# Banded attention, first batch: the mask is put into the PSUM banks by a product with the identity

## The chip, the cores and the metric

One NeuronCore of a Trainium2 chip runs the whole program. The metric is the device time of one execution in microseconds (us). PE is TensorE (its weight loads are shown apart as PEld), DVE is VectorE, ACT is ScalarE, POOL is GpSimd; SP issues every DMA.

## The reference

Inputs: `q`, `k`, `v` of 4 batches, 8 heads, 576 positions, 64 values per head, and the weights of two gated layers. In fp32, with scale 1/8:

```
out_d     = softmax(scale * q_d k_d^T) v_d          # q, k, v averaged over groups of 4 positions: 144 positions
out_up    = each row of out_d repeated 4 times
scores    = scale * q k^T, and -1e9 where |i - j| >= 4
out_local = softmax(scores) v                       # softmax: subtract the row's maximum, exp, divide by the sum
x   = (out_up + out_local), heads side by side      # 2304 x 512
x   = (sigmoid(x w_gate) * (x w_val)) w_out         # layer 1, 512 -> 1536 -> 512
h   = x w_in ;  y = (h * sigmoid(1.702 h)) w_out    # layer 2, 512 -> 2048 -> 512
```

## The kernel before

The kernel records operations (`op`: engine, assumed duration, function, what it reads and writes, a due time) and a planner (`Plan.order`) then lists them. It keeps a clock for each engine, takes the operation of the earliest due time among those whose inputs it believes ready, and so fixes the order in which each engine executes. Each engine works strictly in that order; semaphores make it wait for data. Where the planner believes TensorE idle at the start, it puts in fillers (`warm`, 128x128 bf16 products into a bank that nobody holds, L1173), until the first products of the gated layer's second half. PSUM banks for the attention are handed out by the planner when the first operation that writes one is listed, and given back when its last reader is done. In the first batch six banks serve (`pa` x2, `acc` x4); later batches have only the two `pa`.

**Attention** goes in 16 jobs, one for a batch and a pair of heads; jobs 0 to 3 are the first batch. A job has five parts:

- *scores* (L525): 576 queries lie as 24 tiles of 24 (+8) queries, each against 30 keys; 48 small fp32 products fill two banks (one per head) with 128 x 6 x 30 scores. DVE adds the mask out of SBUF into `sc`, one bank at a time (L532), takes the maximum over both heads (L540), subtracts it (L541); ACT takes exp (L543); DVE sums, divides and transposes into `tt` (L544 to L552).
- *down* (L565): the scores of the averaged positions (`qd`, `kd` from POOL, L493 and L495) in two more banks, maximum on DVE (L572), exp on ACT (L580) and division (L594) into `pd`.
- *down_t* (L609): TensorE transposes `pd`, ACT copies it to `pdt` (L614).
- *values* (L637, L645): products with `v`; ACT copies the averaged part to `up` (L652); DVE adds the two parts into `xf` (L666); ACT and then POOL split it into two fp32r parts, `xhi` and `xlo` (L672, L675). Values read `v` as `vt` (banded) and `vd`, which DVE averages from `vg` (L462, L464), once for two jobs.

**Gated layer 1** then takes x of one batch at a time (L787 to L789, three products for one fp32 product: hi·hi, hi·lo, lo·hi). The weights come packed as 512 KB transfers, are unpacked by ACT and DVE (`we`, L699 to L708) and split into `whi` (ACT, L717) and `wlo` (DVE or POOL, L719). A gated product over one quarter of d_model needs x of one job, so the first block of 128 hidden columns is 4 quarters x 2 matrices x 3 = 24 products of 512 columns, and needs all four jobs. This visit of batch 0 runs beside the attention of batch 1, and so on; layer 2 follows.

The mask is made by POOL at the start, before any recorded operation (L368 to L378). The first operation of the plan for TensorE before the change is job 0's scores.

Of the kernel before, what the change touches and what calls it, by code (L numbers as in the profile page):

```python
# [10 lines left out]
F32 = mybir.dt.float32  # L11
BF16 = mybir.dt.bfloat16
# [5 lines left out]
AX = mybir.AxisListType  # L18

P = 128  # L20
# [41 lines left out]
class Plan:  # L62
# [29 lines left out]
    def op(self, eng, ns, fn, reads=(), writes=(), due=0.0, after=0.0):  # L92
        o = Op()
        o.eng, o.ns, o.fn, o.due, o.n, o.ready = eng, ns, fn, due, len(self.ops), after
        o.fresh, o.bufs = [], set()
        deps = set()
        for group, writing in ((reads, False), (writes, True)):
            for x in group:
                b, part = x if isinstance(x, tuple) else (x, None)
                assert b.some or b.slot.last is b  # L100
                if b.some:
                    o.bufs.add(b)
                    if not b.log:
                        o.fresh.append(b)
                new = True
                for p, q, w in b.log:
                    if (w or writing) and (part is None or q is None or part == q):
                        deps.add(p)
                        new = new and not w
                if new:  # L110
                    for x in b.before:
                        deps.update(e[0] for e in x.log)
        for group, writing in ((reads, False), (writes, True)):
            for x in group:
                b, part = x if isinstance(x, tuple) else (x, None)
                b.log.append((o, part, writing))
        deps.discard(o)
        o.deps = deps
        self.ops.append(o)
        return o  # L120
# [97 lines left out]
def tile_multiscale_attention_gated_ffn(  # L218
# [9 lines left out]
    nc = tc.nc  # L228
    B, NHP, _, S = qT.shape
    D = 64  # L230
# [20 lines left out]
    NQ, NU = 24, 30  # L251
    NT = S // NQ
    NG = NT // 4
# [3 lines left out]
    sb = ctx.enter_context(tc.tile_pool(name="sb", bufs=1))  # L257
# [5 lines left out]
    op, buf = plan.op, plan.buf  # L263
# [76 lines left out]
    def bank(some):  # L340
        banked.append(Buf(None, some))
        return banked[-1]
# [21 lines left out]
    for s in pslots:  # L364
        nc.vector.memset(s.t, 0.0)
    mask = sb.tile([P, NG, NU], F32, name="mask", tag="mask")
    band = sb.tile([P, NU], F32, name="band", tag="band")
    nc.gpsimd.memset(band, 0.0)  # L368
    for i in range(4):
        quarter = band[32 * i:32 * i + 32]  # L370
# [1 line left out]
                                fill=NEG, base=0, channel_multiplier=-1)  # L372
        nc.gpsimd.affine_select(out=quarter, in_=quarter, pattern=[[-1, NU]], compare_op=ALU.is_ge,
                                fill=NEG, base=6, channel_multiplier=1)
    nc.gpsimd.tensor_copy(mask, band[:, None, :].to_broadcast([P, NG, NU]))
    nc.gpsimd.affine_select(out=mask[:32, 0], in_=mask[:32, 0], pattern=[[1, NU]], compare_op=ALU.is_ge,
                            fill=NEG, base=-3, channel_multiplier=0)
    nc.gpsimd.affine_select(out=mask[96:, NG - 1], in_=mask[96:, NG - 1], pattern=[[-1, NU]],  # L378
                            compare_op=ALU.is_ge, fill=NEG, base=S + 2 - NQ * (NT - 1), channel_multiplier=0)
    ident = Buf(Slot(sb.tile([P, P], F32, name="ident", tag="ident")))  # L380
    op("pool", 650.0, lambda: make_identity(nc, ident.t), [], [ident], -10.0e3)


    def act_ns(n, psum=False):
        return (126.0 if psum else 190.0) + n / 1.2

    def dve_ns(n, two=False):
        return 69.0 + n / (1.92 if two else 0.96)
# [78 lines left out]
    class Job:  # L467
# [45 lines left out]
        def scores(self):  # L513


            ss = [bank(self.banks) for _ in range(2)]
            qt, kt, sc, pt, tt, nm, sm = self.qt, self.kt, self.sc, self.pt, self.tt, self.nm, self.sm

            def pe():
                for t in range(NT):  # L520
                    g, i = divmod(t, 4)
                    t = NG * i + g
                    for h in range(2):
                        hs = slice(h * D, (h + 1) * D)
                        nc.tensor.matmul(ss[h].t[32 * i:32 * i + 32, g * NU:(g + 1) * NU],  # L525
                                         qt.t[hs, NQ * t:NQ * t + 32], kt.t[hs, NQ * t:NQ * t + NU],
                                         start=True, stop=True, tile_position=(h * D, 32 * i))

            n = NG * NU
            op("pe", 1500.0, pe, [qt, kt], [*ss, (sc, 0), (sc, 1)], self.due(0.1))  # L530
            for h in range(2):
                op("dve", dve_ns(n), lambda h=h: nc.vector.tensor_add(  # L532
                    sc.t[:, h], ss[h].t[:, :n].rearrange("p (g c) -> p g c", c=NU), mask),
                   [ss[h]], [(sc, h)], self.due(0.1))

            def spread(x):
                return x.t[:, :, :, None].to_broadcast([P, 2, NG, NU])

            at = self.due(0.15)
            op("dve", dve_ns(2 * n), lambda: nc.vector.reduce_max(nm.t, sc.t, axis=AX.X), [sc], [nm], at)  # L540
            op("dve", dve_ns(2 * n), lambda: nc.vector.tensor_sub(sc.t, sc.t, spread(nm)), [nm], [sc], at)  # L541
            p = pt.t[:, :, :, :NU]
            op("act", act_ns(2 * n), lambda: nc.scalar.activation(p, sc.t, AF.Exp, scale=SCALE), [sc], [pt], at)  # L543
            op("dve", dve_ns(2 * n), lambda: nc.vector.reduce_sum(sm.t, p, axis=AX.X), [pt], [sm], at)  # L544

            def inv():
                nc.vector.tensor_scalar_add(sm.t, sm.t, 1.0e-9)
                nc.vector.reciprocal(sm.t, sm.t)

            op("dve", 305.0, inv, [], [sm], at)  # L550
            op("dve", dve_ns(2 * n), lambda: nc.vector.tensor_mul(p, p, spread(sm)), [sm], [pt], at)
            op("dve", 700.0, lambda: nc.vector.transpose(  # L552
                out=tt.t.rearrange("p h g c -> p (h g c)"), in_=pt.t.rearrange("p h g c -> p (h g c)")),
               [pt], [tt], at)
# [659 lines left out]
```

## Time and profile before

| | us |
|---|---|
| three runs | 967.15, 971.45, 972.13 (median 971.45) |
| the profiled execution | 964.45 |
| its span, first to last instruction | 962.6 |
| TensorE busy | 938.1 (97%) |
| DVE busy | 738.5 (77%) |
| ACT busy, POOL busy | 503.5 (52%), 347.4 (36%) |

The profiled execution lies 7.0 us under the median of the three runs. About 1.9 us of it lie outside the span. All times of rows are us from the first instruction. TensorE is busy nearly throughout; the exception is the start, where it also runs fillers. Products are pipelined, so a row's duration of one is longer than the distance to the next.

### The profile page before, as it was taken

How to read it: one execution, taken by the hardware profiler on the slowest of the kernel's cores; microseconds unless marked ns; L12 is line 12 of the kernel's file. 1: busy time of each engine (PE TensorE's matmuls, PEld its weight loads, DVE VectorE, ACT ScalarE, POOL GpSimd, SP SyncE). 2: the span in 40 equal slices, each digit the busy share in tenths (PEclk: the TensorE clock that was granted, in tenths of full speed). 3: DMA queues.
4: the chain of work that ended last, by engine and by line, in shares of the span. 5: the costliest groups of instructions: out<-in, count | busy, mean ns of one | idle time of the engine just before them, and what ended most of it. 6: DMA issues, size and time to landing. Idle time of an engine off the chain costs nothing.

```text
span 962.6 us, 20541 instructions
## 1 busy us (share of the span) xinstructions
PE 938.1 (97%) x8188; PEld 799.3 (83%) x8188; DVE 738.5 (77%) x1350; ACT 503.5 (52%) x1124; POOL 347.4 (36%) x324
## 2 busy tenths in 40 slices
PE   6899999999999999999999999999999999999997
PEld 6687777877778877799788887889898989899896
DVE  6799999776676877455769769998889888876553
ACT  3556566455454555565554465555545554544442
POOL 4321103433233432244755445344435423422220
PEclk8799999999999999999999999999999999999999
DMA  9847548263255532030353012102000200100000
GB/s 220 210 141 216 193 154 216 78 181 113 78 155 176 145 113 99 12 110 1 100 175 121 12 44 76 35 1 67 23 1 1 72 7 1 55 1 1 22 22 23
DMA packets 41071, 83.56 MB, mean 87 GB/s; under 512 B 4184, under 2 KB 15888, under 8 KB 40976
## 3 DMA queue, kind: packets, MB, share of 16 engines
q1 hardware_dynamic: 40976, 82.26, 28.7%
q8 instruction: 64, 1.05, 0.5%
q14 instruction: 31, 0.25, 0.1%
HBM read 66.77 MB, written 15.47 MB: 85 GB/s over the span
## 4 chain that ended last, share of the span: by engine, by line
PE 84%; DVE 10%; issue 2%; DMA 2%; ACT 1%; SPq 0%; POOL 0%; ACTq 0%; DVEq 0%
PE ph L787 12%; PE ph L788 12%; PE ph L789 12%; PE acc L787 11%; PE acc L789 11%; PE acc L788 11%; PE pa L787 3%; PE pa L789 3%; PE pa L788 3%; PE pa L637 2%; DVE wlo L719 1%; PE pa L525 1%; DMA w<-w 1%; DVE th L939 1%; PE pa L565 1%
## 5 line engine op out<-in xcount | busy, mean ns | idle before, releaser
L719 POOL TENSOR_TENSOR wlo<-wr,whi 128x512 fp32r<-128x512 f32 x84 | 117.2, 1395 | 259.1 <-ACT whi L717 192.4
L787 PE MATMUL ph<-xhi,whi 128*128 128x512 f32 (+1 forms) x480 | 181.9, 379 | 1.0 <-DVE th L835 1.0
L788 PE MATMUL ph<-xhi,wlo 128*128 128x512 f32 (+1 forms) x480 | 177.9, 371 | 0.0
L789 PE MATMUL ph<-xlo,whi 128*128 128x512 f32 (+1 forms) x480 | 177.2, 369 | 0.0
L719 POOL TENSOR_TENSOR wlo<-w,whi 128x512 fp32r<-128x512 f32 x70 | 94.9, 1355 | 144.9 <-ACT whi L717 137.6
L717 ACT CAST whi<-w 128x512 fp32r<-128x512 f32 x145 | 89.2, 616 | 74.0 <-PE ph L789 22.4
L717 ACT CAST whi<-wr 128x512 fp32r<-128x512 f32 (+1 forms) x160 | 91.3, 574 | 48.7 <-PE pa L789 16.8
L787 PEld LDWEIGHTS ph<-xhi,whi 128*128 128x128 f32 x480 | 90.5, 189 | 20.5 <-issue 5.7
L789 PEld LDWEIGHTS ph<-xlo,whi 128*128 128x128 f32 x480 | 90.7, 189 | 15.6
L788 PEld LDWEIGHTS ph<-xhi,wlo 128*128 128x128 f32 x480 | 90.7, 189 | 14.7 <-DVE wlo L719 0.7
L787 PE MATMUL acc<-ghi,whi 128*128 128x512 f32 (+1 forms) x240 | 90.6, 378 | 1.0 <-ACT ev L982 1.0
L788 PE MATMUL acc<-ghi,wlo 128*128 128x512 f32 (+1 forms) x240 | 88.8, 370 | 0.2 <-DVE wlo L719 0.2
L789 PE MATMUL acc<-glo,whi 128*128 128x512 f32 (+1 forms) x240 | 88.4, 368 | 0.0
L835 DVE SCALAR_TENSOR_TENSOR th<-th,ph 128x512 f32<-128x512 f32 (+1 forms) x68 | 41.1, 604 | 58.7 <-PE ph L789 45.8
L910 DVE TENSOR_TENSOR w<-pa,w 128x256 f32<-128x256 f32 x128 | 53.5, 418 | 24.3 <-PE pa L789 22.3
L787 PE MATMUL ph<-w,whi 128*128 128x256 f32 x224 | 63.2, 282 | 2.8 <-ACT w L915 2.8
L787 PE MATMUL pa<-xhi,whi 128*128 128x256 f32 x224 | 63.6, 284 | 1.8 <-DVE w L910 1.8
L788 PE MATMUL ph<-w,wlo 128*128 128x256 f32 x224 | 63.4, 283 | 0.1
L789 PE MATMUL ph<-w,whi 128*128 128x256 f32 x224 | 63.2, 282 | 0.0
L789 PE MATMUL pa<-xlo,whi 128*128 128x256 f32 x224 | 63.2, 282 | 0.0
L788 PE MATMUL pa<-xhi,wlo 128*128 128x256 f32 x224 | 63.2, 282 | 0.0
L719 DVE TENSOR_TENSOR wlo<-w,whi 128x512 fp32r<-128x512 f32 x75 | 53.3, 711 | 12.3 <-ACT whi L717 12.2
(161 smaller groups left out, 2335.1 us busy)
## 6 DMA issues: line engine op xcount, KB each, us to landing
w<-w SPq DMA_DIRECT2D x68, 512.0 KB
w2d<-we SPq DMA_DIRECT2D x23, 256.0 KB
qt<-qT SPq DMA_DIRECT2D x16, 288.0 KB
kt<-kT SPq DMA_DIRECT2D x16, 288.0 KB
vg<-v SPq DMA_DIRECT2D x16, 288.0 KB
x2d<-ev SPq DMA_DIRECT2D x16, 256.0 KB
st<-x2d SPq DMA_DIRECT2D x16, 256.0 KB
wr<-w2d SPq DMA_DIRECT2D x16, 256.0 KB
```

The source lines that it names most:

```text
L525: nc.tensor.matmul(ss[h].t[32 * i:32 * i + 32, g * NU:(g + 1) * NU], qt.t[hs, NQ * t:NQ * t + 32], kt.t[hs, NQ * t:NQ * t + NU], start=Tru ...
L565: nc.tensor.matmul(ss[h].t[:GH, r * G:(r + 1) * G], qd.t[h * D:(h + 1) * D, r * GH:(r + 1) * GH], kd.t[h * D:(h + 1) * D, :], start=True, ...
L637: nc.tensor.matmul(s.t[h * D:(h + 1) * D, q:q + NQ], vt.t[ks, g, v0 + h * D:v0 + (h + 1) * D], tt.t[ks, h, g, :NQ], start=True, stop=True, ...
L717: op("act", act_ns(n), lambda: nc.scalar.copy(vh(), vm()), [rm], [rh], due)
L719: op(eng, ns, lambda: on.tensor_sub(vl(), vm(), vh().bitcast(F32)), [rm, rh], [rl], due)
L787: nc.tensor.matmul(o, lhi, rhi, start=first, stop=False, skip_group_check=more)
L788: nc.tensor.matmul(o, llo, rhi, start=False, stop=False, skip_group_check=more)
L789: nc.tensor.matmul(o, lhi, rlo, start=False, stop=last, skip_group_check=more)
L835: op("dve", dve_ns(n), lambda: nc.vector.scalar_tensor_tensor(th.t[:, :n], th.t[:, :n], 1.0, hb[-1].t[:, :n], op0=ALU.add, op1=ALU.mult), ...
L910: op("dve", dve_ns(H), lambda: nc.vector.tensor_add(tq()[:, o], b.t[:, :H], tq()[:, i]), [b, (tmp, i)], [(tmp, o)], t)
L939: op("dve", dve_ns(m), lambda tv=tv, x=x: nc.vector.scalar_tensor_tensor(tv(), tv(), 1.0, x(), op0=ALU.add, op1=ALU.mult), rx, w_, t)
```

## The change

For the first batch alone, each job first puts the mask into its two banks: a product of a bf16 identity with a bf16 copy of the mask (128x180, `start=True`). The 48 score products then add onto it (`start=False`). DVE no longer adds the mask: it takes the maximum from each bank, and subtracts it while it reads the bank a second time. The other batches keep the old way. POOL makes the mask in place (`band` is now a part of `mask`, and the copy is done in two), and makes the identity and the bf16 copy ahead of everything recorded.

```diff
-    band = sb.tile([P, NU], F32, name="band", tag="band")
+    band = mask[:, 1]
...
-    nc.gpsimd.tensor_copy(mask, band[:, None, :].to_broadcast([P, NG, NU]))
+    nc.gpsimd.tensor_copy(mask[:, 0], band)
+    nc.gpsimd.tensor_copy(mask[:, 2:], band[:, None, :].to_broadcast([P, NG - 2, NU]))
...
+    mb = [sb.tile([P, n], BF16, name=nm, tag=nm) for nm, n in (("identb", P), ("maskb", NG * NU))]
+    make_identity(nc, mb[0])
+    nc.gpsimd.tensor_copy(mb[1].rearrange("p (g c) -> p g c", c=NU), mask)
...
-                                         start=True, stop=True, tile_position=(h * D, 32 * i))
+                                         start=bool(b), stop=True, tile_position=(h * D, 32 * i),
+                                         skip_group_check=not b)
...
+            if not b:
+                def first():
+                    for x in ss:
+                        nc.tensor.matmul(x.t[:, :n], mb[0], mb[1], start=True, stop=True)
+
+                op("pe", 260.0, first, [], ss, self.due(0.0))
             op("pe", 1500.0, pe, [qt, kt], [*ss, (sc, 0), (sc, 1)], self.due(0.1))
-            for h in range(2):
+            for h in range(2) if b else ():
                 op("dve", dve_ns(n), lambda h=h: nc.vector.tensor_add(
...
+            for h in range(2) if not b else ():
+                op("dve", dve_ns(n), lambda h=h: nc.vector.reduce_max(
+                    nm.t[:, h], ss[h].t[:, :n].rearrange("p (g c) -> p g c", c=NU), axis=AX.X),
+                   [ss[h]], [(nm, h)], at)
+            for h in range(2) if not b else ():
+                op("dve", dve_ns(n), lambda h=h: nc.vector.tensor_sub(
+                    sc.t[:, h], ss[h].t[:, :n].rearrange("p (g c) -> p g c", c=NU),
+                    nm.t[:, h, :, None].to_broadcast([P, NG, NU])), [ss[h], (nm, h)], [(sc, h)], at)
```

The planner lists everything anew. Below, line numbers of the changed kernel are 5 to 21 higher than those of before.

TensorE's first instructions before: 43 fillers, job 0's 48 score products (banks `pa`) and at once its averaged scores (banks `acc`).

```order
L1173 LDWEIGHTS warm
L1173 MATMUL acc_158<-warm 128x128
...
L525 MATMUL pa_161<-kt_122,qt_120 32x30
L525 MATMUL pa_162<-kt_122,qt_120 32x30
...
L565 MATMUL acc_155<-kd_135,qd_133 72x144
L565 MATMUL acc_156<-kd_135,qd_133 72x144
```

TensorE's first instructions now: the mask products of jobs 0, 1 and 2 (banks `pa_161` to `acc_158`), then 29 fillers, then job 0's scores.

```order
L539 LDWEIGHTS identb
L539 MATMUL pa_161<-maskb,identb 128x180
...
L539 MATMUL pa_162<-maskb,identb 128x180
...
L539 MATMUL acc_155<-maskb,identb 128x180
...
L539 MATMUL acc_156<-maskb,identb 128x180
...
L539 MATMUL acc_157<-maskb,identb 128x180
...
L539 MATMUL acc_158<-maskb,identb 128x180
L1194 LDWEIGHTS warm
L1194 MATMUL ph_160<-warm 128x128
```

The six attention banks now belong to jobs 0 to 2 from the first instruction on, and TensorE's first instruction reads what POOL makes last.

ACT at the start before: the second unpacking (`we_87`) stands ahead of job 0's `pdt`.

```order
L580 ACTIVATE pd_143,smd_147<-acc_155,nmd_145 72x144 x2
L580 ACTIVATE pd_143,smd_147<-acc_156,nmd_145 72x144 x2
L594 ACTIVATE pd_143<-pd_143,smd_147 72x144 x4
L699 ACTIVATE we_87<-w_83 128x512
L614 COPY pdt_149<-acc_155 72x288
L614 COPY pdt_149<-acc_156 72x288
L543 ACTIVATE pt_128<-sc_126 128x12x30
```

ACT at the start now, the same stretch and a little more.

```order
L601 ACTIVATE pd_143,smd_147<-pa_161,nmd_145 72x144 x2
L601 ACTIVATE pd_143,smd_147<-pa_162,nmd_145 72x144 x2
L564 ACTIVATE pt_128<-sc_126 128x12x30
L615 ACTIVATE pd_143<-pd_143,smd_147 72x144 x4
L601 ACTIVATE pd_144,smd_148<-pa_161,nmd_146 72x144 x2
L601 ACTIVATE pd_144,smd_148<-acc_155,nmd_146 72x144 x2
L564 ACTIVATE pt_127<-sc_126 128x12x30
L615 ACTIVATE pd_144<-pd_144,smd_148 72x144 x2
L635 COPY pdt_149<-pa_161 72x288
L635 COPY pdt_149<-acc_155 72x288
L615 ACTIVATE pd_144<-pd_144,smd_148 72x144 x2
L720 ACTIVATE we_87<-w_83 128x512
```

Exp of jobs 1 and 2 now comes ahead of job 0's `pdt`, and job 0's averaged scores use the `pa` banks, which its banded scores held first.

DVE now, from the average of the second pair's values (`vg`) to job 3's subtraction:

```order
L467 TENSOR_TENSOR vg_131<-vg_131 72x2x512
L568 TENSOR_SCALAR sm_141<-sm_141 128x12
L569 RECIPROCAL sm_141<-sm_141 128x12
L469 TENSOR_TENSOR vd_138<-vg_131 72x512
L572 TENSOR_TENSOR pt_127<-pt_127,sm_141 128x12x30
L593 TENSOR_REDUCE nmd_145<-acc_157 72x2
L593 TENSOR_REDUCE nmd_145<-acc_158 72x2
L556 TENSOR_REDUCE nm_140<-pa_162 128x6
```

Behind them stand job 3's second maximum and its two subtractions, and only then job 0's `xf`. Before the change, job 0's `xf` stood ahead of this `vg`. On TensorE the last half of job 3's values now has 15 of the first block's 24 gated products ahead of it (3 before), and the averaged scores of job 4, which followed the 24, stand ahead of the last 6.

## Rows read from the trace of the kernel before

**Rows 1.** The page: DMA busy tenths in 40 slices of the span

```profile
DMA  9847548263255532030353012102000200100000
```

**Rows 2.** Stretches: length, busy us (records) of PE, PEld, DVE, ACT, POOL; clock, DMA, GB/s

```profile
12.28:24.11 11.83, 8.26 (x254) 7.40 (x254) 9.71 (x27) 4.96 (x18) 2.52 (x4) 0.64 1.02 215
24.11:41.62 17.51, 14.59 (x381) 12.28 (x380) 12.61 (x33) 9.18 (x35) 8.16 (x12) 0.77 0.93 228
...
52.70:56.10 3.40, 3.40 (x9) 2.65 (x9) 3.40 (x6) 1.29 (x3) 2.21 (x2) 0.50 0.51 159
...
60.00:70.00 10.00, 10.00 (x45) 8.26 (x44) 9.97 (x21) 4.92 (x9) 3.26 (x4) 1.00 0.56 191
...
100.00:150.00 50.00, 49.06 (x594) 38.41 (x593) 49.20 (x105) 30.98 (x73) 2.93 (x4) 1.00 0.49 164
```

**Rows 3.** Timeline of TensorE: start, us, what, records [idle before <- releaser]

```profile
0.99 4.42 PE L1173 MATMUL acc<-warm 128*128 128x128 bf16 x43 [0.99 <-DVE kt L360]
5.33 1.02 PE L525 MATMUL pa<-kt,qt 64*32 64x30 f32 x96
...
15.18 0.75 PE L525 MATMUL acc<-kt,qt 64*32 64x30 f32 x48 [2.90 <-issue]
...
26.33 1.28 PE L637 MATMUL acc<-tt,vt 30*64 30x24 f32 x40 [2.22 <-issue]
...
29.11 1.17 PE L609 MATMUL acc<-ident,pd 72*72 72x72 f32 x8
...
32.41 0.89 PE L637 MATMUL acc<-tt,vt 30*64 30x24 f32 x48
...
35.16 0.68 PE L1173 MATMUL ph<-warm 128*128 128x128 bf16 x9
...
42.78 0.74 PE L645 MATMUL pa<-pdt,vd 72*64 72x144 f32 x3 [1.16 <-issue]
...
50.57 0.50 PE L787 MATMUL ph<-xhi,whi 128*128 128x512 f32 x1
...
59.05 0.71 PE L565 MATMUL pa<-kd,qd 64*72 64x144 f32 x8
```

**Rows 4.** Timeline of POOL

```profile
3.71 0.21 POOL L378 TENSOR_SCALAR_AFFINE_SELECT mask<-mask 32x30 f32<-32x30 f32 x1
...
4.88 0.29 POOL masks.py:199 TENSOR_SCALAR_AFFINE_SELECT ident<-ident 128x128 f32<-128x128 f32 x1
...
22.42 1.00 POOL L493 TENSOR_TENSOR half<-kt 128x288 f32<-128x288 f32 x1 [0.38 <-DMA kt<-kT]
...
53.69 2.21 POOL L675 TENSOR_TENSOR xlo<-xf,xhi 128x288 fp32r<-128x288 f32 x2 [4.65 <-ACT xhi L672]
```

**Rows 5.** Timeline of DVE

```profile
9.36 0.52 DVE L541 TENSOR_TENSOR sc<-sc,nm 128x360 f32<-128x360 f32 x1
...
13.10 1.22 DVE L462 TENSOR_TENSOR vg<-vg 72x1024 f32<-72x1024 f32 x1 [2.67 <-DMA vg<-v]
...
30.03 1.34 DVE L462 TENSOR_TENSOR vg<-vg 72x1024 f32<-72x1024 f32 x1 [1.00 <-DMA vg<-v]
...
33.89 0.58 DVE L552 STREAM_TRANSPOSE tt<-pt 128x384 f32<-128x384 f32 x1
...
52.68 0.76 DVE L666 TENSOR_TENSOR xf<-acc,up 128x288 f32<-128x288 f32 x2 [0.50 <-PE acc L637]
```

**Rows 6.** Timeline of ACT

```profile
19.54 0.67 ACT L699 ACTIVATE we<-w 128x512 f32<-128x512 f32 x1 [1.08 <-DMA w<-w]
```

**Rows 7.** Groups by line and shape, 0 to 50 us: count | busy us, mean ns | idle before

```profile
L541 DVE TENSOR_TENSOR sc<-sc,nm 128x360 f32<-128x360 f32 x4 | 2.1, 522 | 0.0
...
L540 DVE TENSOR_REDUCE nm<-sc 128x12 f32<-128x360 f32 x4 | 2.1, 518 | 0.1
...
L572 DVE TENSOR_REDUCE nmd<-acc 72x2 f32<-72x288 f32 x4 | 1.7, 444 | 0.0
...
L532 DVE TENSOR_TENSOR sc<-acc,mask 128x180 f32<-128x180 f32 x5 | 1.6, 331 | 0.3 <-PE acc L525 0.3
```

More of the change, by code (lines that the diff above doesn't have):

```diff
@@ L526, in pe @@
                                          qt.t[hs, NQ * t:NQ * t + 32], kt.t[hs, NQ * t:NQ * t + NU],
-                                         start=True, stop=True, tile_position=(h * D, 32 * i))
-            n = NG * NU
+                                         start=bool(b), stop=True, tile_position=(h * D, 32 * i),
+                                         skip_group_check=not b)
+            b, n = self.b, NG * NU
+            if not b:
[3 more added lines that the diff above has]
+                op("pe", 260.0, first, [], ss, self.due(0.0))
             op("pe", 1500.0, pe, [qt, kt], [*ss, (sc, 0), (sc, 1)], self.due(0.1))
-            for h in range(2):
+            for h in range(2) if b else ():
                 op("dve", dve_ns(n), lambda h=h: nc.vector.tensor_add(
@@ L539, in scores @@
             at = self.due(0.15)
-            op("dve", dve_ns(2 * n), lambda: nc.vector.reduce_max(nm.t, sc.t, axis=AX.X), [sc], [nm], at)
-            op("dve", dve_ns(2 * n), lambda: nc.vector.tensor_sub(sc.t, sc.t, spread(nm)), [nm], [sc], at)
+            if b:
+                op("dve", dve_ns(2 * n), lambda: nc.vector.reduce_max(nm.t, sc.t, axis=AX.X), [sc], [nm], at)
+                op("dve", dve_ns(2 * n), lambda: nc.vector.tensor_sub(sc.t, sc.t, spread(nm)), [nm], [sc], at)
+            for h in range(2) if not b else ():
[6 more added lines that the diff above has]
+                    nm.t[:, h, :, None].to_broadcast([P, NG, NU])), [ss[h], (nm, h)], [(sc, h)], at)
             p = pt.t[:, :, :, :NU]
```

## The prediction

> **What bounds the kernel now.** I read the page's slices first, then stretches, then TensorE's timeline, then the other engines around its waits. From about 56 us on, TensorE is the bound: between 60 and 70 us it starts 44 to 45 products of 512 columns, one each 0.227 us without a gap, and from 100 to 150 us it is busy for 49.06 of 50 us, while DVE with 49.20 of 50 has nearly as much to do [rows 2]. What comes before is another regime. DMA is full in the first slices (24 us each) [rows 1], TensorE fills its time with fillers, and the first block of gated products starts at 50.57 us and its 24 are done at 59.05 [rows 3]. As the work behind that mark is the same in both kernels and TensorE does it without gaps, the change is worth what it shifts this mark, plus what it takes from DVE's queue behind it. So I price the start-up alone.
>
> Inside it, three things gate. Data: DVE waits for the values of the first pair of jobs until 13.10 and of the second pair until 30.03 [rows 5]; POOL gets job 2's keys at 22.42 [rows 4]; ACT waits at 19.54 for the second weight block, with job 0's `pdt` behind it [rows 6]. Instructions: TensorE stands still three times for nothing that the profile shows, 2.90, 2.22 and 1.16 us, 6.28 us in all [rows 3]. Between the first and second of these it executes 254 + 254 recorded instructions, between the second and third 381 + 380, close to two and three times 256 (some records are missing) [rows 2]; so I read them as waits for the next piece of its program, while DMA is at 0.93 to 1.02 [rows 2]. Order: everything else is a chain between TensorE, DVE and ACT.
>
> The Trainium skill ("Runtime: NRT & Kernel Launch", Instruction fetch mechanics) says that instructions come in blocks of 256, the next fetched while one is executed, and that crossing a boundary is mostly hidden. The trace agrees on the 256 and not on the hiding: three crossings cost 6.28 us [rows 3].
>
> **The change part by part.**
>
> *DVE work.* One job before: two additions of 331 ns, one maximum of 518, one subtraction of 522 [rows 7]: 1.70 us. Now two subtractions out of a bank, the shape and sources of the addition, 331 each, and two maxima of 180 elements out of a bank. The trace has none of these; the nearest is 444 ns for 288 elements out of a bank, and nothing with 180 elements should be dearer, so 331 to 444, and I take 331, the bank operation of the same size. Together 1.32 (to 1.55): 0.15 to 0.38 us less a job, 0.6 to 1.5 us less for four jobs.
>
> *TensorE's start.* It now waits for POOL. The mask was ready at 3.92; the extra copy, the bf16 identity (about 0.5, as for the fp32 one that ends at 5.17) and the cast bring the first product to about 5.1 us [rows 4]. Six mask products at 0.145 (0.103 for a 128-column filler, 43 in 4.42 us [rows 3], times 180/128) are 0.9, and 29 fillers are 3.0: job 0's scores start at 9.0 instead of 5.33, 3.7 us later. Their subtraction ends at 10.0 + 4 x 0.33 = 11.4 instead of 9.88 [rows 5]. What hides this: the values at 13.10 and job 2's keys at 22.42, whose transfers have the same bytes ahead of them in both kernels. Without that cover it costs 1.5 to 3.7 us.
>
> *Banks.* The six banks are taken at once, so job 0's averaged scores wait for its subtractions, and job 1's transposes for those of job 3, behind which they stand. DVE's row there is: `vg` at 30.03, two maxima of averaged scores, `vd`, division, then job 3's maxima and subtractions. Before, a similar row (a sum and a transpose in place of the four) ran from 30.03 to 34.47 [rows 5]; exchanging 0.94 us for four times 0.27 gives 34.6. Job 1's transposes, at 29.11 before [rows 3], start at 34.6: 5.5 us later. In return job 3's scores and subtractions are done by then; before, they followed.
>
> *From there to job 3's `xf`.* Before: 29.11 to 52.68 is 23.6 us, with 69 fillers (about 5.7 us at 0.065 to 0.104 each) and the 1.16 us wait. Now 12 more gated products stand in it (15 instead of 3), 35 fillers fewer, job 3's scores are gone and its averaged scores come in. An upper figure keeps all waits: 23.6 - 35 x 0.083 + 12 x 0.227 + about 0 = 23.4, so `xf` at 58.0. A lower one is TensorE's own work without a wait: three times a job's values, 2.75 us (32.41 to 35.16, six fillers in it [rows 3]), 15 x 0.227 = 3.4, and about 5.2 for three sets of transposes, two of scores and the other fillers: 16.9, so `xf` at 51.5. I take 55.5, nearer to the upper end, because of the waits that the row of before holds. It is 2.8 us later than the 52.68 of before [rows 5].
>
> *From `xf` to the end of the 24.* ACT and POOL split it: from 52.68 to 55.90 [rows 4, 5], 3.2 us, the same now, on the path in both. After it, before had 14 products left (55.90 to 59.05 = 3.15 us); now 6, that is 1.4. So the mark falls at 55.5 + 3.2 + 1.4 = 60.1, with job 4's averaged scores done already, which before came after the mark and took 0.71 [rows 3]. 60.1 against 59.76: **+0.3 us**, between -3.7 and +2.8. The 16 fillers there lie in the wait for the split.
>
> *Behind the mark.* DVE is ahead: where job 3's sum is listed, five first unpackings are done and four splits, against four and two before, some 3 us of DVE work. TensorE loses 0.94 us to idleness from 100 to 150 us [rows 2]; I give back half of it, -0.5 (0 to -1). POOL's and SP's later exchanges of neighbours I cost at nothing, as TensorE is the bound there and their buffers are ahead; without that cover up to 1 us either way.
>
> Sum: +0.3 - 0.5 = **-0.2 us** on the 964.45 us of the profiled execution. That execution is 7.0 us under the median of the three runs, and the four together scatter by 7.7 us with a mean of 968.8. The forecast of a median is therefore 968.8 - 0.2, rounded to **969 us**: no change that can be told. About 0.5%, 4.9 us, is what a measurement of this kernel can tell from no change.
>
> **Rivals.**
>
> 1. *The start-up gets really shorter.* For: before, 10 of the first products ran between 52.70 and 56.10 at 0.50 of the clock, the 1.2 GHz level [rows 2], at about 0.43 us each instead of 0.227; with more gated products ahead TensorE works more evenly, and might be at the 2.4 GHz level there (-2.0). Weight blocks are unpacked earlier. If `xf` comes at 52.5, the mark moves by -2.7, the clock gives -1 more for what is left, and DVE's lead a full -1: -4.7 to -5.5, **964**. The rule of the Trainium skill cited above ("Runtime: NRT & Kernel Launch", Instruction fetch mechanics), crossings mostly hidden, would do this. Against: three crossings weren't hidden, and TensorE crosses as many now. 0.18.
> 2. *The banks tie TensorE's order to DVE's, and the late start is not absorbed* (the side of slower). Job 3's scores must be done by 33.9, when DVE comes to their maximum. Without a wait for instructions they end near 27.8 (keys at 22.42, scores 0.9, 19 fillers 2.0, transposes, averaged scores, scores). Two such waits (2.2 and 2.9) bring that to 32.9; with the 3.7 us of the late start in the same fetches it is 36.6, and all behind it shifts by 2.7. With the upper figure for the rest (+2.5) and +0.3: +5.5, **974 to 975**. It decides if job 3's scores end after 33.9. For: the fetches are TensorE's own pace, and it starts late. Against: it needs every wait on the path. 0.20.
> 3. *Nothing changes, since the same transfers gate*: that is the forecast. 0.62.
>
> **How the numbers follow.** Forecast 0.62, its own range 965 to 973 (the mark's -3.7 to +2.8, DVE's 0 to -1). The 80% range reaches into both rivals and takes in the scatter of runs: 962 to 976. Faster by over 0.5%: 0.18 and a little of the forecast's edge, 0.20; slower: 0.18, as rival 2 at its smaller price stays within; same: 0.62.
>
> **What would show it.** Right: TensorE's first product near 5.1 us and job 0's scores near 9.0; DVE's second `vg` again near 30; job 1's transposes near 34.6; job 3's `xf` between 53 and 58; the 24th product near 60; from there an unbroken row at 0.227 us. Wrong in size: the maxima out of a bank far from 331 ns; `vg` landing elsewhere; a different number of unexplained waits on TensorE between 10 and 50 us. Wrong in kind: a time off by over 5 us with the mark within 2 us of 59.8, which would put the difference behind the start-up.

## Result: 973.46 us, about 5 us slower

| | before | changed |
|---|---|---|
| median (runs) | 967.92 us (14) | 973.46 us (14) |
| lowest to highest | 966.07 to 972.66 | 969.42 to 980.97 |
| profiled execution, its span | 964.45, 962.6 | 973.61, 971.8 |
| ratio | 1 | 1.0052, 95% interval 1.0035 to 1.007 |

The interval of the ratio excludes 1, that is, no change. The forecast was 969 us, no difference that can be told, in a range of 962 to 976; the range holds the time, but a difference clear of the noise came where none was forecast.

The page of the changed kernel answers to [rows 1]: engines first, then DMA in 40 slices. TensorE is the bound as before.

```profile
PE 943.2 (97%) x8195; PEld 802.3 (83%) x8195; DVE 731.7 (75%) x1350; ACT 504.6 (52%) x1124; POOL 349.0 (36%) x328
...
DMA  8735746273354622130263002101000200100000
```

TensorE's timeline, the columns of [rows 3]. The first product comes when POOL's bf16 mask is there. Three waits that the view puts down to nothing ("issue") follow, 8.60 us together, 6.28 before. The last row is the first product behind the 24, the "mark" of the prediction.

```profile
4.88 0.46 PE L539 MATMUL pa<-maskb,identb 128*128 128x180 bf16 x2 [4.88 <-POOL maskb L384]
...
8.96 1.21 PE L530 MATMUL pa<-kt,qt 64*32 64x30 f32 x96
...
16.98 0.34 PE L530 MATMUL acc<-kt,qt 64*32 64x30 f32 x26 [3.99 <-issue]
...
28.83 0.21 PE L530 MATMUL acc<-kt,qt 64*32 64x30 f32 x1 [1.46 <-issue]
...
35.13 0.19 PE L658 MATMUL acc<-tt,vt 30*64 30x24 f32 x1 [3.15 <-issue]
...
36.96 0.69 PE L630 MATMUL pa<-ident,pd 72*72 72x72 f32 x4
...
48.05 0.80 PE L808 MATMUL ph<-xhi,whi 128*128 128x512 f32 x1
...
66.83 0.50 PE L808 MATMUL ph<-xhi,whi 128*128 128x512 f32 x1
```

DVE, to set beside [rows 5]: job 0's maxima and differences, the second pair of values, job 3's differences, and job 0's and job 3's `xf`.

```profile
10.23 0.60 DVE L556 TENSOR_REDUCE nm<-pa 128x6 f32<-128x180 f32 x2 [1.87 <-PE pa L530]
10.74 0.59 DVE L560 TENSOR_TENSOR sc<-pa,nm 128x180 f32<-128x180 f32 x2
...
27.63 1.22 DVE L467 TENSOR_TENSOR vg<-vg 72x1024 f32<-72x1024 f32 x1 [0.39 <-DMA vg<-v]
...
31.65 0.33 DVE L560 TENSOR_TENSOR sc<-acc,nm 128x180 f32<-128x180 f32 x1
...
36.52 0.46 DVE L687 TENSOR_TENSOR xf<-pa,up 128x288 f32<-128x288 f32 x1 [4.20 <-PE acc L658]
...
62.82 0.76 DVE L687 TENSOR_TENSOR xf<-pa,up 128x288 f32<-128x288 f32 x2 [0.60 <-PE pa L658]
```

Groups, 0 to 60 us, as in [rows 7]: a maximum or a difference straight out of a bank takes what the addition took (331 ns).

```profile
L556 DVE TENSOR_REDUCE nm<-acc 128x6 f32<-128x180 f32 x5 | 1.6, 332 | 0.3 <-PE acc L530 0.3
L560 DVE TENSOR_TENSOR sc<-acc,nm 128x180 f32<-128x180 f32 x5 | 1.5, 330 | 0.0
```

Stretches, the columns of [rows 2]. From 36 us to the mark TensorE has no pause, and the granted clock stays at 0.50, the 1.2 GHz level, until 58.4.

```profile
36.00:58.40 22.40, 22.40 (x400) 18.49 (x397) 14.67 (x35) 12.62 (x40) 7.77 (x10) 0.50 0.34 94
60.00:70.00 10.00, 10.00 (x130) 7.37 (x123) 9.36 (x20) 5.90 (x13) 3.15 (x4) 1.00 0.58 193
100.00:150.00 50.00, 49.33 (x558) 38.55 (x556) 49.51 (x106) 31.37 (x73) 3.51 (x4) 1.00 0.57 181
```

**A trap in this comparison.** The 25th gated product starts at 66.83 us, in the profile of before at 59.70, as if all the loss and more lay ahead of it. But that profile was of an execution (964.45) faster than any of the 14 above. A second one of the same kernel (e8 below) has it at 66.95 and takes 972.43 us:

```profile
14.66 0.75 PE L525 MATMUL acc<-kt,qt 64*32 64x30 f32 x48 [3.11 <-issue]
...
22.47 0.63 PE L637 MATMUL acc<-tt,vt 30*64 30x24 f32 x15 [1.29 <-issue]
...
31.62 1.28 PE L637 MATMUL acc<-tt,vt 30*64 30x24 f32 x40 [5.86 <-issue]
...
66.95 0.50 PE L787 MATMUL ph<-xhi,whi 128*128 128x512 f32 x1
```

Here the wait that [rows 3] show with 2.22 us took 5.86, and the waits together 10.26, more than in the changed kernel, so their sum does not set the two kernels apart. The clock was at 0.50 where the first execution had 1.00 (first row: the second execution; second: the first):

```profile
22.00:45.90 23.90, 17.57 (x431) 14.90 (x431) 12.31 (x33) 7.08 (x26) 8.05 (x12) 0.50 0.73 178
```

```profile
32.20:42.40 10.20, 8.72 (x307) 7.39 (x305) 9.10 (x23) 6.19 (x26) 4.39 (x6) 1.00 0.88 215
```

The clock goes with the time from one execution to the next: the 14 of the changed kernel run from 969.42 us, with a mean granted clock of 0.987, to 980.97 us, with 0.973 (a delay in the part at 0.50 also lowers the mean, so this does not say which brings which). It is not what the change costs: the mean over the 14 is 0.982, over 129 executions of the kernel before, beside the experiments below, 0.981.

So one execution's start says little, but from that product to the end kernels of one order agree within about 1 us (the table has one exception, e10). The experiments are therefore read by medians, and split there: "tail" is the span less the start of the 25th product; "start" is the median less the tail and less what lies outside the span, so an estimate of where that product starts in a median run.

### The profile page after: what moved, and what is told of

The parts are those of the page before. It is cut to its first block, busy times and chain, and to the rows that moved or that the text cites. A ratio compares the mean times of both kernels' runs of the same rounds, so it can differ in the third digit from the quotient of the medians.

```text
span 971.8 us, 20564 instructions
## 1 busy us (share of the span) xinstructions
PE 943.2 (97%) x8195; PEld 802.3 (83%) x8195; DVE 731.7 (75%) x1350; ACT 504.6 (52%) x1124; POOL 349.0 (36%) x328
## 4 chain that ended last, share of the span: by engine, by line
PE 80%; DVE 12%; issue 3%; DMA 2%; ACT 2%; POOL 1%; SPq 0%; POOLq 0%; ACTq 0%; DVEq 0%
PE ph L808 11%; PE acc L808 10%; PE ph L809 10%; PE ph L810 10%; PE acc L810 10%; PE acc L809 10%; PE pa L808 3%; PE pa L810 3%; PE pa L809 3%; PE pa L658 2%; DMA w<-w 2%; DVE wlo L740 2%; PE pa L530 1%; PE ph L1194 1%; DVE we L724 1%
```

## The experiments

All times in us; ratios are to the kernel before on the same chip, with 95% intervals, and differ a little from the quotients of the medians. Each experiment ran 12 times, but e9 10, e10 9 and e7 6 times. The kernel before, run beside them, had medians of 968.83, 968.38, 969.01 and 969.89 (with e1 to e4, e5 to e8, e9 to e12, e13 to e16). "Order" is the order of instructions on every engine, with the banks that the planner hands out in it.

| kernel | order | median | ratio | tail | start |
|---|---|---|---|---|---|
| before (e8's reference) | old | 968.38 | | 902.9 | 63.6 |
| e8 before again | old | 970.35 | 1.0003 (0.998 to 1.0025) | 903.7 | 64.9 |
| e4 wide fillers | old | 970.03 | 1.0009 (0.9992 to 1.0026) | 903.5 | 64.8 |
| e5 late start | old | 969.12 | 1.0004 (0.9977 to 1.0031) | 903.5 | 63.9 |
| e11 few fillers | old | 969.87 | 1.0011 (0.9996 to 1.0025) | 904.1 | 64.0 |
| e13 new arithmetic | old | 969.74 | 1.0001 (0.9983 to 1.0019) | 902.9 | 65.1 |
| e14 36 more fillers | old | 972.08 | 1.0016 (0.9999 to 1.0034) | 904.1 | 66.2 |
| the changed kernel | new | 973.46 | 1.0052 (1.0035 to 1.007) | 905.0 | 66.7 |
| e3 wide fillers | new | 971.74 | 1.0032 (1.0011 to 1.0053) | 904.7 | 65.2 |
| e6 29 fillers fewer | new | 971.98 | 1.0043 (1.0017 to 1.007) | 904.6 | 65.6 |
| e7 36 more fillers | new | 979.94 | 1.0117 (1.008 to 1.0154) | 905.1 | 72.5 |
| e9 old arithmetic | new | 973.85 | 1.0048 (1.0028 to 1.0068) | 904.4 | 67.4 |
| e10 few fillers | new | 976.09 | 1.0061 (1.0039 to 1.0083) | 906.8 | 67.5 |
| e1 mask in the score operation | third | 970.61 | 1.0002 (0.9978 to 1.0026) | 901.2 | 67.6 |
| e2 mask ready at 3.9 us | fourth | 968.10 | 0.9983 (0.9961 to 1.0005) | 900.9 | 65.1 |
| e12 e2, few fillers | fourth | 970.26 | 1.0017 (1.0005 to 1.003) | 902.3 | 65.9 |
| e15 less to transfer | new | 969.48 | 0.9996 (0.9979 to 1.0013) | 904.7 | 63.0 |
| e16 less to transfer | old | 967.85 | 0.9985 (0.9965 to 1.0005) | 903.0 | 63.0 |

**e1 and e2: TensorE not late.** e1 puts the mask's products into the score operation:

```diff
             def pe():
+                if not b:
+                    for x in ss:
+                        nc.tensor.matmul(x.t[:, :n], mb[0], mb[1], start=True, stop=True)
...
-                op("pe", 260.0, first, [], ss, self.due(0.0))
-            op("pe", 1500.0, pe, [qt, kt], [*ss, (sc, 0), (sc, 1)], self.due(0.1))
+            op("pe", 1500.0 if b else 1760.0, pe, [qt, kt], [*ss, (sc, 0), (sc, 1)], self.due(0.1))
```

e2 leaves them apart but tells the planner when the mask is ready:

```diff
-                op("pe", 260.0, first, [], ss, self.due(0.0))
+                op("pe", 260.0, first, [], ss, self.due(0.0), 3900.0)
```

> The changed kernel, but each job's mask product stands right before its 48 score products, in the same planned operation: TensorE starts with 43 fillers as before the change, no bank is taken ahead, the arithmetic is the changed kernel's. Theory 1 (claiming six banks early makes job 0's averaged scores and job 1's transposes late): 967 to 969 us, job 3's xf below 56 us. Theory 2 (TensorE's late start and the fetch waits that follow from it): also 967 to 969. Theory 3 (the way through the banks itself, mask by product and two readings by DVE, costs it): 973, xf again near 62.

> The changed kernel with the mask products declared ready only at 3.9 us of the planner's clock: TensorE runs 35 fillers first and need not wait for POOL, while the products stay operations of their own that take banks ahead of the scores (four at once). Theory 1 (early claims): still 971 to 974. Theory 2 (late start): 967 to 969, with the first wait for instructions ending near 15.2 as before the change and not at 17.0.

Both take the loss back, and I first read this as proof that the late start was the cause. The table shows otherwise: their starts (67.6 and 65.1) are no earlier than those of the old order, their tails are 2 to 3 us shorter. Both edits change the planner's order all the way to the end. One place of e1, between products 1729 and 2000 where layer 2 takes over, against e8 (length, then TensorE busy): 0 us of idle time there instead of 2.02. Another is the stretch from the 25th product to product 500, 129.7 us instead of 131.6.

```profile
473.13:533.30 60.17, 60.17 (x273) 50.05 (x272) 53.04 (x63) 34.27 (x68) 40.97 (x33) 1.00 0.47 153
```

```profile
474.67:537.60 62.93, 60.91 (x273) 49.96 (x272) 50.27 (x61) 33.32 (x66) 39.41 (x33) 1.00 0.45 142
```

**e3 and e4: fillers of 512 columns** in the new and the old order.

```diff
-    WARM_N = 128
-    WARM_NS = 110.0
+    WARM_N = 512
+    WARM_NS = 440.0
...
-            x.t[:, :WARM_N], warm, warm[:, :WARM_N], start=True, stop=True)
+            x.t[:, :WARM_N].rearrange("p (a c) -> p a c", c=P), warm,
+            warm[:, None, :].to_broadcast([P, WARM_N // P, P]), start=True, stop=True)
```

> The changed kernel with fillers of 512 columns counted at 440 ns instead of 128 at 110: the same filler time, a quarter of the instructions, some 240 fewer records ahead of job 3's last values, and at the 2.4 GHz level the planned filler time is also the real one half of the time only, as before. Theory 4 (waits for the next 256 instructions): the waits of 3.99, 1.45 and 3.15 us shrink to below 5 us in all, 968 to 970. Theory 1 or 5 (the clock at 1.2 GHz from 31 to 58 us): no gain, 972 to 975.

> The kernel before the change with the same wide fillers. Theory 4: its three waits of 6.3 us shrink, 963 to 966, faster than both. If the waits are hidden behind DVE and the transfers: 967 to 969.

The new order stays 0.3% slower, the old one shows no difference that can be told.

**e5 and e6: lateness without the order, the order without lateness.** e5 lets TensorE wait for its fillers' zeros until 4.25 us in the old order, by writing these on POOL behind the mask:

```diff
-    nc.vector.memset(warm, 0.0)
...
+    nc.gpsimd.memset(warm, 0.0)
```

e6 drops the 29 fillers ahead of job 0's scores:

```diff
+    skip, warms = 29, list(plan.fillers.values())
     for o in plan.order():
+        if skip and any(o is x for x in warms):
+            skip -= 1
+            continue
         o.fn()
```

> The kernel before with one memset moved: the zeros of the filler products' tile are written by POOL behind the mask, so that TensorE's 43 fillers start near 4.3 us and job 0's scores near 8.7 us, as late as in the changed kernel (8.96), while the order of every engine's instructions is the old one and the mask is added by VectorE. Theory A (the late start of the scores is the cost, whatever the order behind it): 971 to 974 us, a ratio of 1.003 to 1.006, and the 25th gated product starts near 65 to 67 us instead of 59.7. Theory B (the planner's new order in the first 100 us is the cost, and the late start is absorbed while the first transfers land): 968 to 970 us, a ratio within 0.998 to 1.002, and the 25th gated product near 61 to 64 us.

> The changed kernel without the 29 filler products that stand between the mask's products and job 0's scores; the order of everything else stays the changed kernel's. Job 0's scores can then start near 5.6 us instead of 8.96, if kt and qt have landed. Theory A (late scores): 968 to 970 us, a ratio within 0.998 to 1.002, the whole loss taken back. Theory B (the new order): 972 to 974 us, a ratio of 1.003 to 1.006 as before, and gated products 73 to 145 again take about 22.3 us.

e5 starts its scores at 8.91, as late as the changed kernel, and loses nothing that can be told; e6 starts them at 5.87 and is as slow as the changed kernel.

```profile
4.25 4.73 PE L1173 MATMUL acc<-warm 128*128 128x128 bf16 x43 [4.25 <-POOL warm L379]
8.91 1.02 PE L525 MATMUL pa<-kt,qt 64*32 64x30 f32 x96
```

```profile
5.87 1.21 PE L530 MATMUL pa<-kt,qt 64*32 64x30 f32 x96
```

Theory A, the late start as the whole cost, falls.

**e7 and e14: 36 fillers more in front**, in the new and the old order; all behind them stays. The edit of e7 (e14 has such a loop in front of job 0's score products):

```diff
+                    for _ in range(0 if self.hp else 36):
+                        nc.tensor.matmul(ss[0].t[:, :P], warm, warm, start=True, stop=True)
```

> The changed kernel with 36 more filler products in front of the mask's first product, so that TensorE is busy from 1.0 us, and its 256-record steps fall 36 products earlier in the work; job 0's scores stay near 9.0 us and the order of all else stays. Theory A (late scores) and theory B (new order) both expect no gain: 972 to 974 us, a ratio of 1.003 to 1.006. A third, C (what costs is where the instruction fetches of TensorE fall, since the first record block ends later when TensorE idles until 4.9 us): the first fetch wait ends near 14 instead of 17.0 us, no wait of 3 us in job 0's values near 32 us, and 968 to 970 us.

> The kernel before with 36 more fillers ahead of job 0's scores, which so start near 9 us; each of TensorE's 256-record steps then falls 36 products earlier in the work. A late start alone cost nothing in this order (e5, ratio 1.0004). Theory C (where the steps fall in the work decides, since the fetch there waits 2 to 6 us while the queues are full): a change of over 2 us in either direction, as the same 36 fillers made in the new order (973.5 to 979.9 us). Rival (the old order absorbs it): 967 to 970 us, a ratio of 0.998 to 1.002.

e7 came out as no theory had it, 979.94. As C said, the first wait ends at 14.21; but one of 6.22 us now stands in job 0's values:

```profile
14.21 0.87 PE L530 MATMUL acc<-kt,qt 64*32 64x30 f32 x62 [3.24 <-issue]
...
33.23 0.30 PE L660 MATMUL pa<-tt,vt 30*64 30x24 f32 x2 [6.22 <-issue]
```

e14 (its scores start at 6.75, not near 9) is slower by 0.16%, with an interval that just includes no change; its median lies 2.19 us above that of the kernel before. By the ratio the rival fits, by the medians theory C: e14 does not decide.

**e8: before again.**

> The kernel before, unchanged, with a second profile of its own. Every theory: a ratio within 0.998 to 1.002. What it is for: the profiled execution of before took 964.45 us, below all but the fastest of its runs, and the start of an execution nearer to the median is wanted to compare with. If the first profile was a lucky one, the 25th gated product starts later here than 59.7 us, near 61 to 64 us, with a longer stretch of the lower clock before 58 us; if it was typical, it starts at 59.5 to 60 us again.

The ratio is as expected. The start of the 25th product, 66.95, is later than expected: this is the trap above.

**e9 and e13: order and arithmetic exchanged.** e9 keeps the new order on every engine, but emits no mask product, and adds the mask on DVE inside the operation that takes the maximum:

```diff
                 def first():
-                    for x in ss:
-                        nc.tensor.matmul(x.t[:, :n], mb[0], mb[1], start=True, stop=True)
+                    pass
...
+            def most(h):
+                nc.vector.tensor_add(sc.t[:, h], ss[h].t[:, :n].rearrange("p (g c) -> p g c", c=NU), mask)
+                nc.vector.reduce_max(nm.t[:, h], sc.t[:, h], axis=AX.X)
```

e13 keeps the old order; in the first batch its score operations write the mask into the banks first, and the operation that added the mask now does this:

```diff
...
+                nc.vector.reduce_max(nm.t[:, h], z, axis=AX.X)
+                nc.vector.tensor_sub(sc.t[:, h], z, nm.t[:, h, :, None].to_broadcast([P, NG, NU]))
...
```

Here `z` is the bank; the two operations over 360 columns stay in the plan and do nothing in the first batch. In the traces ACT executes in e9 the list of the changed kernel, and in e13 that of the kernel before.

> The changed kernel's order on every engine, with the old arithmetic in it: the mask's products are left out, and where VectorE took the maximum from a bank it adds the mask into SBUF and takes the maximum there, as before. TensorE is rid of 8 products (1.2 us before the mark) and starts with fillers at 1 us. Theory B (the planner's new order is the cost): 971 to 974 us, a ratio of 1.003 to 1.006, and from the 25th gated product to the end 904.4 to 905.1 us, as in the changed kernel (before: 903.5). Theory M (the products by the mask and their wait are the cost): 967 to 970 us, a ratio within 0.998 to 1.002.

> The kernel before in its own order on every engine, with the changed arithmetic in it: each of job 0 to 3's score blocks is led by the two products that write the mask into its banks, VectorE takes maximum and difference straight from the banks where it added the mask, and the two instructions over 360 columns behind it fall away. Theory B (only the order cost the 5 us): 966 to 970 us, a ratio of 0.997 to 1.001, and from the 25th gated product to the end 903.5 us as before. Rival (the way through the banks costs by itself): 971 to 974 us, a ratio of 1.002 to 1.006.

This decides it. The new order with the old arithmetic is as slow as the changed kernel (1.0048), the old order with the new arithmetic as fast as before (1.0001), and the two intervals don't meet. The way through the banks costs nothing and gives nothing that can be told (its interval reaches 0.2% either way); the order that the planner made of it costs the 5 us.

**e10, e11, e12: few fillers.** Behind job 1's or 2's scores they are left out (87, 110 and 108 before the 25th product). e10:

```diff
+    keep, warms = 84, list(plan.fillers.values())
     for o in plan.order():
+        if any(o is x for x in warms):
+            keep -= 1
+            if keep < 0:
+                continue
         o.fn()
```

e11 keeps 62, in the kernel before, and e12 69, in e2.

> The changed kernel without its fillers from job 1's second scores on: 84 of 171 fillers before the mark stay, 87 go, which take 8 to 9 us there at 95 to 106 ns each. Theory F (from 32 us to the mark TensorE's own queue is the bound, so what is put into it delays the mark one for one, whether fetch wait, filler or mask product): the mark 4 to 8 us earlier than 66.8, and 966 to 970 us, a ratio of 0.998 to 1.002. Rival (values, xf and the first batch's other chains are the bound and the fillers only fill waits): 972 to 974 us, a ratio of 1.003 to 1.006. A slower result would mean that the fillers hold TensorE's clock up.

> The kernel before without its fillers behind job 1's scores: 62 of 172 stay, 110 go (about 11 us of TensorE's time before the mark, at 93 to 106 ns). Theory F (TensorE's queue is the bound from about 32 us to the mark): the mark 3 to 8 us earlier than 60 to 67, and 961 to 966 us, a ratio of 0.993 to 0.998. Rival (fillers fill waits alone): a ratio within 0.998 to 1.002. Against the changed kernel with as few fillers, both on the same chip: the difference of the two that stays is what the change costs without fillers, 5 us if it is the order, 1 to 2 us if it is the crowding of TensorE's queue.

> The version of the changed kernel whose mask products the planner takes for ready at 3.9 us (968.1 us, and from the 25th gated product to the end 900.9 us against 903.5 of before), without its fillers from job 2's scores on. Theory F: its start gains as the others do, 961 to 966 us, a ratio of 0.992 to 0.998, the best of all. Rival (fillers fill waits alone): 967 to 969 us, a ratio of 0.997 to 1.001.

No kernel gains, though about 10 us of fillers are gone, so theory F's forecast fails; e12 is slower than the kernel before by 0.17%, and its interval excludes no change. But the clock went down with the fillers: the mean over all executions from 0.982 to 0.977 in the changed kernel (e10), from 0.981 to 0.974 in the kernel before (e11), from 0.984 to 0.975 in e2 (e12). The runs change both at once, and what the fillers take from TensorE's queue by themselves stays open. New and old order keep their distance (976.09 to 969.87).

**e15 and e16: less to transfer at the start.** Four of the first five loads of `w` bring an eighth of their columns; DVE fills the rest with zeros at the start.

```diff
...
-        op("sp", P * 4096, lambda: nc.sync.dma_start(out=w.t, in_=src), [], [w], at, after)
+        z = slice(0, 64 if (layer, f, part) in CUT else None)
+        op("sp", P * 4096, lambda: nc.sync.dma_start(out=w.t[:, z], in_=src[:, z]), [], [w], at, after)
```

> The changed kernel with four of the first five loads of w cut to an eighth of their columns (the rest of these tiles is zeros; their products are wrong), 1.8 MB less of the 8.9 MB ahead of 40 us. Theory C (fetch waits under full queues make the new order dear): its waits fall from 8.6 us together to under 4 us, and its distance to the kernel before that is cut in the same way falls from 5 us to 1 to 2 us, the part behind the 25th gated product. Theory D (the order's dependencies alone): the distance stays 4 to 6 us. By itself: 964 to 972 us.

> The kernel before with the same four loads cut to an eighth of their columns. Both theories: 962 to 968 us, faster than before by what the fuller queues cost it; it is what e15 is compared with. Theory C: its fetch waits fall from 6 to 10 us together to under 4 us.

With 7.19 MB instead of 8.99 ahead of 40 us, the new order is only 1.63 us behind the old, and all of that is tail (904.7 to 903.0); the starts are alike. The waits of e15, 6.41 us, are shorter than the 8.60, but not under the 4 that were expected:

```profile
17.03 0.35 PE L535 MATMUL acc<-kt,qt 64*32 64x30 f32 x26 [4.07 <-issue]
...
28.08 0.21 PE L535 MATMUL acc<-kt,qt 64*32 64x30 f32 x1 [0.54 <-issue]
...
32.74 0.19 PE L663 MATMUL acc<-tt,vt 30*64 30x24 f32 x1 [1.80 <-issue]
```

Those of e16 are 3.48:

```profile
15.84 0.76 PE L530 MATMUL acc<-kt,qt 64*32 64x30 f32 x48 [1.44 <-issue]
...
26.25 1.28 PE L642 MATMUL acc<-tt,vt 30*64 30x24 f32 x40 [2.04 <-issue]
```

This speaks against D, where the distance stays, but is not proof: the difference of the two ratios, 0.0011, is uncertain by about 0.0026 (both intervals' half-widths, added in squares), which reaches to 3.6 us; and fewer bytes also let values and weights land earlier. Nor does it show that the waits of C are the cause: the profiled execution of e16 (964.31 us) is 3.5 us faster than its median, so its 3.48 us may not be typical.

## Why the prediction was wrong

**Right: the edit itself.** Maxima and differences out of a bank were taken at 331 ns; they took 332 and 330. TensorE's first product was put at 5.1 (4.88), job 0's scores at 9.0 (8.96), its subtraction's end at 11.4 (11.3, by the rows of DVE). That the late start is absorbed was argued from the transfers, and e5 and e6 show it, within e5's interval (0.9977 to 1.0031). e13 shows that saving DVE work in the first batch is worth nothing that can be told: 1.0001 (0.9983 to 1.0019).

**Wrong by little, in both directions.** The second `vg` was put near 30 and came at 27.63; job 3's subtractions were put at 34.6 and ended at 31.98. Job 1's transposes were put at 34.6 and started at 36.96, no longer held by the banks but by the wait that ends at 35.13 in the values ahead of them.

**The step that failed first: "From there to job 3's `xf`".** Predicted 55.5, 20.9 us behind the transposes; measured 62.82, 25.9 us behind them, outside its bounds of 51.5 and 58.0. TensorE had no pause on this path, so what failed is the price of its own work, put at 16.9 us without a wait: it took the whole 25.9. The rows for that price came from an execution with the clock at 1.00 from 32.2 to 42.4 us. The changed kernel's was at 0.50 up to 58.40, for 21.4 of the 25.9 us; in e8 the old order, too, was at 0.50 to 45.9, and its job 3's `xf` came at 60.05 instead of 52.68:

```profile
60.05 0.75 DVE L666 TENSOR_TENSOR xf<-acc,up 128x288 f32<-128x288 f32 x2 [1.82 <-PE acc L637]
```

So most of this miss belongs to the execution and not to the change: beside e8 the `xf` is 2.8 us later, as forecast, though e8's execution lies 2.1 us above its median. With the `xf` went the mark: 60.1 forecast, 66.83 measured, 66.7 in a median run. How much of that is the change? By the table, four kernels of the old order that differ little (e4, e5, e8, e13) and the reference start between 63.6 and 65.1, the changed kernel at 66.7 and e9 at 67.4: about 2 to 3 us, where +0.3 was forecast. This is an estimate; e3 and e6, also of the new order, start at 65.2 and 65.6. That the cost is order, and not mask products, fillers or lateness, e9, e10 beside e11, and e5 show. What in the order costs it at the start is not settled: e15 and e16 take it away by taking transfers away, and e7 shows that moving the same work against the record steps moves the median by 6.5 us, though in the old order (e14) by only 1.6 to 2.2. This points to where TensorE's waits for instructions fall in the work while the queues are full, but does not show it; that values and weights land at other times in the new order is not excluded.

**The second: "Behind the mark", -0.5 forecast.** I took the work there as the same and TensorE as gapless, and credited DVE's lead. But the planner's order changes to the very end. The tail is 905.0 against 902.9 and 903.7 in two profiles of before: +1.3 to +2.1. Its largest piece lies over 550 us behind the place of the edit: between products 2500 and 3500, in layer 2, TensorE waits twice for ACT's `w`, 2.9 us in the changed kernel and in e9, 1.8 in e8 (the view of waits, products 2500 to 3500: us in total, times, longest).

```profile
PE ph L808 <- ACT w L936: 2.9, 2, 1.5
```

```profile
PE ph L787 <- ACT w L915: 1.8, 2, 0.9
```

This piece is no chance: the stretch takes 162.0 to 162.4 us in every kernel of the old order, and 163.2 to 164.7 in every one of the new. e1 and e2 take 163.9 and 163.1 there and have the shorter tails by what they gain elsewhere.

2 to 3 and 1.3 to 2.1 make the 5 us, within what such estimates can tell.

**The rivals.** Rival 2 came nearest to the time (974 to 975) by luck, not by its reason. It was to be decided by job 3's scores ending after 33.9; DVE had their differences done at 31.98, so the scores were not late, and that a late start by itself costs the time is refuted by e5 and e6. Rival 1's shorter start did not come. The sentence "a time off by over 5 us with the mark within 2 us" did not apply, as the mark moved as well.

**The forecast's reference.** Setting the sum on 968.8 rather than on the 964.45 of the profile was right: the reference medians are 967.9 to 969.9. It should have led me to distrust the same execution's rows. Three small readings of the prediction are off without effect: by its terms its own range is 964 to 972, not 965 to 973; 8 products, not 10, ran at 0.43 us ahead of 56.10; 13, not 14, were left there.

**Open.** e2 has the lowest median, 968.10, but its interval includes no change; no version here beats the kernel before beyond doubt. A start like that of the old order with a tail like e2's would be about 2 us faster by the table, an estimate; it wasn't built.

## What to carry to other kernels

Where a planner sets the order, an edit's price is that of the whole new order, up to the end of the program, and not that of the instructions edited: exchange order and arithmetic in two runs (e9, e13) before explaining anything by the edit. Take two profiles of each kernel before comparing starts, since the start moved by 7.25 us between two executions of the same kernel. A gain in the median says little of its cause until it is split by place: e1 and e2 seemed to mend the start and gained in the tail.

## What the runs showed of the hardware

- TensorE's waits put down to "issue" end when instructions have come. The DMA records of the traces hold transfers of 16,384 bytes on a queue named `q8 instruction`, 64 in the changed kernel's execution, one for every 256 of TensorE's 16,390 records. In the changed kernel three of them land at 15.43, 27.30 and 33.65 us, and the waits end at 16.98, 28.83 and 35.13, 1.5 us behind each. In all traces the "issue" waits of over 0.5 us on TensorE ahead of 55 us end 1.3 to 1.8 us behind such a landing; the two exceptions, the first waits of e3 and e9, have a cause that the traces don't show.
- In the old order the wait in job 0's values took 2.22, 5.86 (e8), 6.50 (e5) and 2.04 us (e16). It varies with the start of the transfer, which in e8 begins at 28.87 us, 3.1 us after TensorE stopped, and in e16 at 23.60, 0.6 us before it stopped; both take 1.2 to 1.3 us. Why the one begins so late isn't shown. The Trainium skill ("Runtime: NRT & Kernel Launch", Instruction fetch mechanics) calls such crossings mostly hidden; up to 36 us the rows don't agree; from there to 75 us TensorE passes four more steps of 256 records in the changed kernel without a wait over 0.1 us.
- TensorE ran at 0.50 of the clock for 22.4 us without a pause (36.00 to 58.40 above). With 110 fillers fewer (e11) the low level lasted 47.8 us in one piece, TensorE being busy for 33.59 of them, and the median was no different from before that can be told (ratio 1.0011):

```profile
12.10:59.90 47.80, 33.59 (x822) 27.35 (x811) 34.12 (x83) 22.09 (x74) 15.57 (x20) 0.50 0.69 174
```

- So 10 us of fillers fewer together with a longer low level left the time of this kernel as it was. What either is worth alone, these runs don't show.
